# Loading r of the first three chunks on ACT's DMA queue in a recurrent attention and cosine MoE kernel

## The chip, the cores and the metric

The kernel runs on one core of one Trainium2 chip. The metric is the device time of one execution in microseconds. Engines are called PE (matmul), DVE (vector), ACT (activation), POOL (GpSimd) and SP (which only issues DMAs here). DMAs can be issued from the queues of SP, ACT and POOL.

## The reference

Two parts follow one another. The first is a linear recurrence over 768 time steps for 4 batches and 8 heads of width 48, with a decay w and a bonus u:

```python
for t in range(S):
    cur = einsum('bhd,bhe->bhde', u[None] * k[:, :, t], v[:, :, t])
    y[:, :, t] = einsum('bhd,bhde->bhe', r[:, :, t], state + cur)
    state = w[None, :, :, None] * state + einsum('bhd,bhe->bhde', k[:, :, t], v[:, :, t])
```

Its output, 3,072 tokens by 384, is the x of the second part, with weights of 384 x 2,048 and 2,048 x 384:

```python
h = x @ w_in
g = h * cos(h)
return g @ w_out
```

All data are float32, but the weights are drawn as float64 and converted in the kernel.

## The kernel before, in words

**The attention part.** The 768 steps of each batch are cut into chunks of 128; there are 24 chunks, numbered so that chunk i belongs to batch i mod 4. Function `chunk` writes down the operations of one chunk. It loads r, k and v with time on the partitions. POOL forms r*k (line 882), multiplies it by u (line 935), and multiplies k by its decay table (line 892). PE transposes k and r (line 851), DVE and ACT bring them back with decay (lines 910, 921 and 930), PE forms the 128 x 128 scores (line 976), ACT writes the diagonal that comes from u (line 960), DVE puts the scores under a mask (line 981), and PE forms the output with v and the carried state (lines 996 and 1007) and the new state (line 1022). ACT and DVE split the output into a high and a low part, `xh` and `xl` (lines 1222 and 1227). The first 12 chunks (`EARLY`) go this way. The later 12 are loaded and multiplied in another form (`late`), which the change does not touch.

**The buffers of the early chunks.** r has a ring of four buffers (`X_r`), k and v have six each (`R_k` with `X_k`, `R_v` with `X_v`), besides others that all chunks share.

**The MoE part.** Tokens go in eight blocks of three chunks. A step is one block and one of the 16 slices of 128 of the hidden width: nine matmuls for h (line 314), whole periods taken off on ACT and DVE (lines 326 and 329), the cosine with ACT's Sin function (line 332), the product with h (line 1330), a split into high and low (lines 1333 and 1336), and nine matmuls for the output (line 321). Each weight slice is loaded as raw 64-bit words (lines 550 and 571), put together from integers on ACT, DVE and POOL (lines 664 to 695), and split into high and low (lines 705 and 712); function `conv` writes this down. The first twelve chunks make up the first four blocks, and these are worked through four groups of slices.

**What sets the order.** Nothing is issued as it is written down. Every piece of work is given to a planner with `op(engine, due, cost, emit, after, bufs, ...)`. The planner plays the engines through in time with the costs written in the code: on each engine, of the pieces that could start first, it picks the one with the earliest due time. It makes seven passes (`PASSES`), in which due times are replaced by the latest time at which a piece may start, and keeps the pass that ends first by its own reckoning. The resulting order is then fixed on every engine's queue. Pieces that share a `line` are kept in the order in which they are written down, and `behind` keeps a piece behind another. A piece with a `dma` cost also waits for room on a modelled common transfer line. Where PE is to stand idle in the first part by this reckoning, warm-up matmuls are put in (line 1396). `CHUNK_SHIFT` and `TILE_SHIFT` are added to the due times of the 24 chunks and the 32 weight tiles; they were found by a search.

**The queues at the start.** All loads are on SP's queue. It issues w (line 447), then u (line 522), then the chunks' loads: r and k of an early chunk in two halves each (`load_p`, line 781), v in one (line 773). Loads of r, k and v are kept behind u (`behind=o_u`). ACT has nothing to do until it copies the decay table `dec_k` (line 513), except that it runs one Sin on a single element (line 281), which brings its function table in.

Of the kernel before, what the change touches and what calls it, by code (L numbers as in the profile page):

```python
# [14 lines left out]
AF = mybir.ActivationFunctionType  # L15
# [20 lines left out]
ON_DVE = (0, 0, 0)  # L36
RAW_K = 2
EARLY = 12

CHUNK_SHIFT = (  # L40
    -29.5, -37.6, -6.2, -7.2, 3.0, 2.3, 2.1, 0.6, 0.7, 1.4, 4.4, 4.6, -6.7, -104.0, -50.4, 0.8,
    -55.8, -62.5, -102.0, -6.5, -17.7, -92.4, 6.3, -24.8,
)
TILE_SHIFT = (
    -8.6, 5.5, -10.8, -48.0, -4.3, -6.4, -0.2, -16.4, 11.6, -5.1, 12.1, 2.5, 3.8, -0.3, 3.2, -0.8,
    14.0, 22.6, -2.8, 2.9, 12.9, -1.4, -0.8, 53.9, -8.3, 6.4, 1.2, 83.9, -13.0, -11.3, 2.5, 17.4,
)
PASSES = 7
DMA_AHEAD, DMA_FIRST, DMA_LAST, DMA_LAND = 3.0, 1.3, 0.6, 1.95
# [36 lines left out]
class Plan:  # L86
# [9 lines left out]
    def op(self, eng, due, cost, emit, after=(), bufs=(), lat=0.2, line=None, port=False, dma=0.0, behind=None):  # L96

        o = Op(eng, due, cost, lat, emit, after, bufs, self.lines.get(line) if line else behind, port, dma)
        if line:
            self.lines[line] = o  # L100
        self.ops.append(o)
        return o
# [137 lines left out]
def kernel(  # L240
# [11 lines left out]
    nc = tc.nc  # L252
# [25 lines left out]

    tiny = const.tile([1, 1], F32, name="tiny")
    nc.vector.memset(tiny, 0.0)  # L280
    nc.scalar.activation(tiny, tiny, AF.Sin)

    ident = const.tile([P, P], F32, name="ident")
    flag = const.tile([1, 1], I32, name="flag")
# [50 lines left out]
    with ExitStack() as actx:  # L335
# [63 lines left out]
        op = plan.op  # L399
        PE, DVE, ACT, POOL, SP, ACTQ = "PE", "DVE", "ACT", "POOL", "SP", "ACTQ"  # L400
# [33 lines left out]
        def wr():  # L434
# [15 lines left out]
            lat=2.6,  # L450
# [13 lines left out]
                )  # L464

        op(PE, -300, 2.4, start_banks, [o_dve], b_0)

        o_wT = op(PE, -95, 0.2, lambda: nc.tensor.transpose(b_w()[:, 0:NP], b_row()[0:NP, 0 : 2 * DP], ident[0:NP, 0:NP]), [o_w, o_wr, o_pool], [b_w, b_row], lat=0.3)

# [41 lines left out]
        def tab_copy():  # L511
# [6 lines left out]
        o_u = op(  # L518
            SP,
            -23.9,  # L520
            0.5,
            lambda: nc.sync.dma_start(u_b.rearrange("p h d -> p (h d)"), u.rearrange("h d -> (h d)").partition_broadcast(P)),
            lat=2.0,
            dma=0.6,
            behind=o_w,
        )
# [226 lines left out]
        def chunk(i, due, xbuf):  # L753
            b, c = i % B, i // B
            first = i < RAW_K
            bk = B_EARLY if i < EARLY else B_ATT

            def on(which):
                return (DVE, 0.47, nc.vector) if i < ON_DVE[which] else (POOL, 1.05, nc.gpsimd)
            mb, ab = Buf(R_f), Buf(R_a)  # L760
            if i < EARLY:
                rb, kb, vb = Buf(X_r), Buf(R_k + X_k), Buf(R_v + X_v)
            else:
                rb, kb, vb = Buf(R_f), Buf(R_k), Buf(R_v)
            trp = Buf(B_TR)
            R_Tc = R_T + X_T if i < EARLY else R_T
            kT, rT = Buf(R_Tc), Buf(R_Tc)
# [4 lines left out]
            def load(buf, src):  # L772
                return lambda: nc.sync.dma_start(
                    buf()[:, :, 0:D], src[b, :, c * C : (c + 1) * C, :].rearrange("h t d -> t h d")
                )


            def load_p(buf, src):
                def go():
                    for j in range(2):  # L780
                        nc.sync.dma_start(  # L781
                            buf()[:, j::2, 0:D],
                            src[b, j * NP : (j + 1) * NP, c * C : (c + 1) * C, :].rearrange("h t d -> t h d"),
                        )

                return go
# [10 lines left out]

            late = i >= EARLY
            if late:
                ks, rs = Buf(R_raw), Buf(R_raw)  # L800

            rbs = [rb]
# [31 lines left out]
            ahead = [last_A[0]] if late else []  # L834
            ln = "late" if late else None
            if late:
                l_ks = op(SP, due - 6.2, 1.9, load_s(ks, k), ahead, [ks], line=ln, dma=1.45)
                l_rs = op(SP, due - 6.1, 1.9, load_s(rs, r), ahead, [rs], line=ln, dma=1.45)
            l_k = op(SP, due - 5.2, 0.5 if late else 1.15, (load if late else load_p)(kb, k), ahead, [kb], line=ln, dma=1.25, behind=o_u)
            l_r = op(SP, due - 5.1, 0.5 if late else 1.15, load_r if late else load_p(rb, r), ahead, rbs, line=ln, dma=1.25, behind=o_u)  # L840
            l_v = op(SP, due - 5.0, 0.6, load(vb, v), ahead, [vb], line=ln, dma=1.25, behind=o_u)


# [52 lines left out]
            if not late:  # L896
# [7 lines left out]
                    lat=0.3,  # L904
# [341 lines left out]
        for i in range(NJ):  # L1246
            n = block_of[i]
            t = i - FIRST[n]
            if i < EARLY:
                due = -1.5 * (EARLY - i) - 1.0  # L1250
            else:
                lo, hi = first_h[n - 1], first_h[n] - 1
                if i >= XS:
                    lo = max(lo, last_h[block_of[i - XS]])
                due = lo + (hi - lo) * (t + 1) / BLOCKS[n]
            due = round(due, 2)
            due += CHUNK_SHIFT[i]
            x_ready.setdefault(n, []).extend(chunk(i, due, xb[i]))
            x_ready_of[i] = x_ready[n][-1]
# [4 lines left out]
        for i in range(2 * NF):  # L1264
            f, part = divmod(i, 2)
            g = max(x for x in group if x <= f)
            if g == 0:
                due = 2 * i - 3.0
            else:
# [3 lines left out]
                due = lo + (hi - lo) * (i - 2 * g + 1) / n_g  # L1273
            due = round(due, 2)
# [16 lines left out]
        for s, (n, f, f0, f1) in enumerate(steps):  # L1291
# [56 lines left out]
            for t in range(nt):  # L1348
# [8 lines left out]
                if f == f1 - 1:  # L1357
# [16 lines left out]
                    def st(ob=ob, dst=dst, f0=f0, last=last):  # L1374
# [14 lines left out]
                        dma=0.6 if f0 == 0 else 1.0,  # L1389
# [160 lines left out]
```

## Time and profile before

| | |
|---|---|
| times of three runs | 511.3, 509.42, 510.1 us |
| median | 510.1 us |
| time of the profiled execution | 510.29 us |
| its span, first to last instruction | 508.7 us |
| mean granted TensorE clock | 0.999 |
| PE busy | 497.1 us (98% of the span) |
| transfers of all queues | 61.82 MB |

The span is the time from the first instruction to the last, and the profiled execution's own time is a little longer. Busy shares are averages over the whole span. "L882" is line 882 of the kernel. A bracket behind an instruction tells how long its engine had stood idle and what ended that, and "SPq" and "ACTq" are the DMA issues on the queues of SP and ACT. [...]

### The profile page before, as it was taken

The page shows a single profiled execution, that of the slowest core. Times are in us where ns is not written, and L with a number is a line of the kernel's source. Part 1 is how long each engine was busy: PE and PEld are TensorE (multiplying, and loading weights), DVE is VectorE, ACT ScalarE, POOL GpSimd, SP SyncE. Part 2 cuts the span into 40 slices and gives each one's busy share as a digit, 9 for nine tenths or more (in the row PEclk, how much of TensorE's full clock was granted, in tenths as well). Part 3 has the DMA queues.
Part 4 walks back from the last instruction along what each step waited for, and adds up shares of the span by engine and source line. Part 5 has one row for each costly group of instructions (what it writes and reads, how often), then busy time and mean ns, then how long its engine had stood idle before and what let it go on. Part 6 is the DMA issues. An engine that isn't in the chain of part 4 may idle for free.

```text
span 508.7 us, 14928 instructions
## 1 busy us (share of the span) xinstructions
PE 497.1 (98%) x5872; PEld 474.7 (93%) x5872; DVE 396.0 (78%) x836; ACT 316.3 (62%) x805; POOL 176.3 (35%) x183
## 2 busy tenths in 40 slices
PE   8998999999999999999999999999999999999995
PEld 6876799999999999999999999999999999999994
DVE  6887888898998889798656678988888865566553
ACT  2886867767676676555755565655766655554443
POOL 6968312245434646364220144443224500000000
PEclk9999999999999999999999999999999999999999
DMA  9978525467946868672543938667765252010001
GB/s 139 158 144 175 136 84 179 165 129 141 178 129 130 181 134 182 123 150 71 111 77 95 156 97 212 151 154 190 189 155 130 75 173 64 0 48 3 0 1 52
DMA packets 116657, 61.82 MB, mean 122 GB/s; under 512 B 80097, under 2 KB 112482, under 8 KB 116578
## 3 DMA queue, kind: packets, MB, share of 16 engines
q1 hardware_dynamic: 110962, 53.11, 43.0%
q0 software_dynamic: 5184, 7.08, 10.1%
q8 instruction: 48, 0.79, 0.7%
q10 hardware_dynamic: 432, 0.59, 0.3%
q14 instruction: 31, 0.25, 0.2%
HBM read 48.96 MB, written 11.80 MB: 119 GB/s over the span
## 4 chain that ended last, share of the span: by engine, by line
PE 88%; SPq 4%; DMA 3%; POOL 3%; issue 1%; ACT 0%; DVE 0%; ACTq 0%; POOLq 0%
PE psum L321 40%; PE psum L314 39%; PE psum L1153 4%; SPq L781 2%; DMA early_r<-in_r_dram 2%; PE psum L1078 1%; PE psum L1094 1%; DMA early_k<-in_k_dram 1%; POOL f L935 1%; POOL f L882 1%; PE psum L1007 1%; DMA k<-in_k_dram 1%; SPq L550 1%; POOL k L892 1%; PE psum L996 1%
## 5 line engine op out<-in xcount | busy, mean ns | idle before, releaser
L321 PE MATMUL psum<-w_out_hi,gh 128*128 128x384 f32 x384 | 131.6, 343 | 0.0
L314 PE MATMUL psum<-xh,w_in_hi 128*128 128x384 f32 x384 | 129.9, 338 | 0.0
L321 PE MATMUL psum<-w_out_hi,gl 128*128 128x384 f32 x384 | 129.3, 337 | 0.0
L321 PE MATMUL psum<-w_out_lo,gh 128*128 128x384 f32 x384 | 129.3, 337 | 0.0
L314 PE MATMUL psum<-xh,w_in_lo 128*128 128x384 f32 x384 | 129.3, 337 | 0.0
L314 PE MATMUL psum<-xl,w_in_hi 128*128 128x384 f32 x384 | 129.0, 336 | 0.0
L1333 ACT CAST gh<-f 128x384 fp32r<-128x384 f32 (+1 forms) x132 | 66.0, 502 | 56.3 <-PE psum L321 33.8
L1336 DVE TENSOR_TENSOR gl<-f,gh 128x384 fp32r<-128x384 f32 (+1 forms) x132 | 83.2, 636 | 20.6 <-ACT gh L1333 20.0
L329 DVE SCALAR_TENSOR_TENSOR f<-psum,qi 128x384 f32<-128x384 f32 (+1 forms) x132 | 71.0, 540 | 34.7 <-ACT qi L326 34.2
L326 ACT ACTIVATE qi<-psum 128x384 int32<-128x384 f32 (+1 forms) x132 | 62.8, 478 | 49.5 <-PE psum L314 48.9
L332 ACT ACTIVATE f<-f 128x384 f32<-128x384 f32 (+1 forms) x132 | 67.5, 513 | 30.7 <-DVE f L329 29.5
L1330 DVE TENSOR_TENSOR f<-psum,f 128x384 f32<-128x384 f32 (+1 forms) x132 | 71.0, 540 | 17.0 <-ACT f L332 14.4
L321 PEld LDWEIGHTS psum<-w_out_hi,gh 128*128 128x128 f32 x384 | 72.0, 188 | 2.0 <-ACT f L1365 0.3
L314 PEld LDWEIGHTS psum<-xh,w_in_hi 128*128 128x128 f32 x384 | 72.1, 188 | 0.8 <-DVE f L329 0.2
L314 PEld LDWEIGHTS psum<-xl,w_in_hi 128*128 128x128 f32 x384 | 72.2, 188 | 0.0
L314 PEld LDWEIGHTS psum<-xh,w_in_lo 128*128 128x128 f32 x384 | 72.2, 188 | 0.0
L321 PEld LDWEIGHTS psum<-w_out_hi,gl 128*128 128x128 f32 x384 | 72.1, 188 | 0.0
L321 PEld LDWEIGHTS psum<-w_out_lo,gh 128*128 128x128 f32 x384 | 72.1, 188 | 0.0
L695 POOL TENSOR_TENSOR f<-f,raw 128x384 int32<-128x384 int32 x32 | 37.2, 1166 | 71.6 <-ACT f L332 19.4
L1380 POOL DMA_DIRECT2D out_dram<-f x36 | 33.6, 1071 | 55.0 <-ACT f L1365 47.4
L870 POOL TENSOR_TENSOR T<-T,decT_k 112x512 f32<-112x512 f32 x12 | 15.6, 1303 | 78.3 <-DVE T L865 70.1
L935 POOL TENSOR_TENSOR f<-f,u_b 128x384 f32<-128x384 f32 x24 | 26.9, 1122 | 0.2
(127 smaller groups left out, 627.8 us busy)
## 6 DMA issues: line engine op xcount, KB each, us to landing
raw<-in_moe_w_out_dram SPq DMA_DIRECT2D x32, 384.0 KB, 3.4
out_dram<-f POOLq DMA_DIRECT2D x36, 192.0 KB, 4.9
raw<-in_moe_w_in_dram SPq DMA_DIRECT2D x96, 64.0 KB, 2.3
raw<-in_moe_w_in_dram SPq DMA_DIRECT2D x16, 384.0 KB, 4.6
raw<-in_k_dram SPq DMA_DIRECT2D x47, 96.0 KB, 3.3
raw<-in_r_dram SPq DMA_DIRECT2D x47, 96.0 KB, 2.8
out_dram<-f SPq DMA_DIRECT2D x21, 192.0 KB, 2.2
v<-in_v_dram SPq DMA_DIRECT2D x18, 192.0 KB, 4.2
```

What stands on the lines that cost most here:

```text
L314: nc.tensor.matmul(ph, a, b_, start=(i == 0), stop=(i == len(mm) - 1))
L321: nc.tensor.matmul(acc, a[:, ts], b_, start=(first and i == 0), stop=(last and i == 2))
L326: nc.scalar.activation(qi, ph, AF.Copy, scale=INV_2PI, bias=0.25)
L329: nc.vector.scalar_tensor_tensor(q, ph, INV_2PI, qi, op0=ALU.mult, op1=ALU.subtract)
L332: nc.scalar.activation(q, q, AF.Sin, scale=TWO_PI, bias=0.5 * math.pi)
L695: lambda: nc.gpsimd.tensor_tensor(ai(), ai(), cn(), op=ALU.add),
L935: e1, due - 2.2, c1, lambda: n1.tensor_tensor(heads(mb), heads(mb), u_b, op=ALU.mult), [o_m, o_u], [mb], port=True
L1153: nc.tensor.matmul(xv()[rows, kk, tokens(n)] if same else apart(rows, kk), lhsT, rhs, start=quadrant not in opened, stop=True, skip_group_ ...
L1330: nc.vector.tensor_tensor(g()[:, cs], ph()[:, cs], q()[:, cs], op=ALU.mult)
L1333: nc.scalar.copy(gh()[:, cs], g()[:, cs])
L1336: nc.vector.tensor_tensor(gl()[:, cs], g()[:, cs], f32(gh())[:, cs], op=ALU.subtract)
L1380: nc.gpsimd.dma_start(dst, ob(), accum_op=ALU.add)
```

## The change

The loads of r for the first three chunks are issued from ACT's queue instead of SP's, in one line (chunk 0, 1, 2), with a due time ahead of everything else. The loads of k for these chunks stay on SP, with a due time 30 us earlier than before, and are no longer kept behind u. The Sin that brings ACT's function table in, which stood at the very start, becomes a piece for the planner that comes behind the r load of the second chunk. The shifts of chunks and tiles were searched anew.

```diff
+BOTH = 3

 CHUNK_SHIFT = (
-    -29.5, -37.6, -6.2, -7.2, 3.0, 2.3, 2.1, 0.6, 0.7, 1.4, 4.4, 4.6, -6.7, -104.0, -50.4, 0.8,
-    -55.8, -62.5, -102.0, -6.5, -17.7, -92.4, 6.3, -24.8,
+    -46.9, -67.3, -0.9, -1.6, 2.9, 1.8, 3.5, 4.5, 6.0, 7.9, 7.7, 9.6, -6.8, -110.2, -76.9, 1.4,
+    -86.2, -21.4, -56.0, -6.5, -17.8, -61.4, 22.7, -32.5,
 )
 TILE_SHIFT = (
-    -8.6, 5.5, -10.8, -48.0, -4.3, -6.4, -0.2, -16.4, 11.6, -5.1, 12.1, 2.5, 3.8, -0.3, 3.2, -0.8,
-    14.0, 22.6, -2.8, 2.9, 12.9, -1.4, -0.8, 53.9, -8.3, 6.4, 1.2, 83.9, -13.0, -11.3, 2.5, 17.4,
+    -2.0, 4.1, -3.5, -56.1, -11.7, -0.5, -11.9, -17.3, 0.8, -2.4, 8.8, 1.7, 4.5, 6.6, 1.3, -1.3,
+    13.1, 14.2, -7.2, 2.4, 12.2, -2.4, -8.6, 51.6, -5.7, 12.5, 4.4, 64.6, -13.1, -12.8, 12.2, 49.0,
 )
...
     nc.vector.memset(tiny, 0.0)
-    nc.scalar.activation(tiny, tiny, AF.Sin)
...
         op(PE, -300, 2.4, start_banks, [o_dve], b_0)
+        o_sin = op(ACT, -150, 1.5, lambda: nc.scalar.activation(tiny, tiny, AF.Sin))
...
-            def load_p(buf, src):
+            def load_p(buf, src, js=(0, 1), eng=nc.sync):
                 def go():
-                    for j in range(2):
-                        nc.sync.dma_start(
+                    for j in js:
+                        eng.dma_start(
                             buf()[:, j::2, 0:D],
                             src[b, j * NP : (j + 1) * NP, c * C : (c + 1) * C, :].rearrange("h t d -> t h d"),
                         )
...
-            l_k = op(SP, due - 5.2, 0.5 if late else 1.15, (load if late else load_p)(kb, k), ahead, [kb], line=ln, dma=1.25, behind=o_u)
-            l_r = op(SP, due - 5.1, 0.5 if late else 1.15, load_r if late else load_p(rb, r), ahead, rbs, line=ln, dma=1.25, behind=o_u)
+            if i < BOTH:
+                l_k = op(SP, due - 35.2, 1.1, load_p(kb, k), [], [kb], dma=1.2)
+                l_r = op(ACT, -300 + i, 1.1, load_p(rb, r, eng=nc.scalar), [], rbs, line="first", dma=0.1, lat=2.0)
+                if i == 1:
+                    o_sin.after.append(l_r)
+            else:
+                l_k = op(SP, due - 5.2, 0.5 if late else 1.15, (load if late else load_p)(kb, k), ahead, [kb], line=ln, dma=1.25, behind=o_u)
+                l_r = op(SP, due - 5.1, 0.5 if late else 1.15, load_r if late else load_p(rb, r), ahead, rbs, line=ln, dma=1.25, behind=o_u)
```

## The prediction

> **What bounds the kernel now.** I read the page's totals first, then the busy time by stretches, then the first 60 us engine by engine.
>
> ```profile
> span 508.7 us, 14928 instructions
> ## 1 busy us (share of the span) xinstructions
> PE 497.1 (98%) x5872; PEld 474.7 (93%) x5872; DVE 396.0 (78%) x836; ACT 316.3 (62%) x805; POOL 176.3 (35%) x183
> ```
>
> The profiled execution took 510.29 us, so 1.59 us lie outside its span. The median of the three runs shown is 510.1, so the sum below is made against 510.29 and stands 0.2 above the median. The 98% for PE is an average and counts warm-up matmuls as busy, so I cut the span where PE's idle gaps end, in the windows view (start:end, length, then each engine's busy us and count, granted clock, DMA share, GB/s):
>
> ```profile
> 0.00:5.80 5.80, 4.69 (x18) 2.42 (x19) 4.13 (x29) 1.49 (x2) 3.50 (x17) 1.00 0.57 109
> 5.80:33.90 28.10, 27.37 (x547) 22.45 (x547) 21.63 (x41) 19.39 (x58) 24.18 (x24) 1.00 1.05 149
> 33.90:59.24 25.34, 21.71 (x523) 17.39 (x519) 20.15 (x42) 20.02 (x59) 14.09 (x14) 1.00 0.82 168
> 59.24:502.60 443.36, 443.34 (x4792) 432.41 (x4792) 349.95 (x726) 274.93 (x687) 134.52 (x128) 1.00 0.50 117
> 502.60:508.70 6.10, 0.03 (x1) 0.00 (x0) 0.11 (x1) 0.48 (x1) 0.00 (x0) 0.89 0.31 107
> ```
>
> From 59.24 to 502.60 PE is busy 443.34 of 443.36 us at full clock. Nothing that moves loads or changes the order can win there, unless work is drawn into the first stage. The last 6.10 us are the final copies and stores, which the diff does not touch. So the change is worth what it does to the first 59.24 us, and a microsecond by which the full stretch starts earlier is a microsecond of the whole.
>
> In that stage PE is idle 59.24 - (4.69 + 27.37 + 21.71) = 5.47 us, and part of its busy time is filler:
>
> ```profile
> L1396 PE MATMUL psum<-warm 128*128 128x256 bf16 x101 | 14.8, 287 | 1.1 <-DVE f L437 1.1
> ```
>
> Warm-ups and idle together are some 20 us. That is what an ideal start could give at most, and it shows that PE does not set the pace. POOL does for a long stretch: three products per early chunk (r*k at L882, times u at L935, k times decay at L892).
>
> ```profile
> 7.22 1.01 POOL L882 TENSOR_TENSOR f<-early_r,k 128x384 f32<-128x384 f32 x1 [2.72 <-DMA k<-in_k_dram]
> 8.31 1.72 POOL L935 TENSOR_TENSOR f<-f,u_b 128x384 f32<-128x384 f32 x1
> 10.00 1.00 POOL L882 TENSOR_TENSOR f<-early_r,k 128x384 f32<-128x384 f32 x1
> 12.04 1.01 POOL L882 TENSOR_TENSOR f<-early_r,k 128x384 f32<-128x384 f32 x1 [1.03 <-DMA k<-in_k_dram]
> ```
>
> ```profile
> 12.04:33.90 21.86, 20.48 (x21) 1.00 0.92 145
> ```
>
> POOL waits 2.72 us for the first k and 1.03 for the third, and from 12.04 to 33.90 it is busy 20.48 of 21.86 us. In that stretch the chunks come out as fast as POOL multiplies. What makes its first and third product start earlier moves this whole stretch; two later waits I come to below.
>
> **The change part by part.** SP's queue now issues w, then u, then r and k in turn (start, length, count):
>
> ```profile
> 0.84 0.38 SPq L447 DMA_DIRECT2D f<-in_w_dram  x1
> 1.27 0.36 SPq L522 DMA_DIRECT2D u_b<-in_u_dram  x1
> 1.68 0.98 SPq L781 DMA_DIRECT2D early_r<-in_r_dram  x2
> 2.70 2.24 SPq L781 DMA_DIRECT2D k<-in_k_dram  x4
> 4.98 2.15 SPq L781 DMA_DIRECT2D early_r<-in_r_dram  x4
> 7.18 1.06 SPq L781 DMA_DIRECT2D k<-in_k_dram  x2
> 8.29 1.13 SPq L781 DMA_DIRECT2D early_r<-in_r_dram  x2
> ...
> 14.37 2.50 SPq L781 DMA_DIRECT2D early_r<-in_r_dram  x2
> ```
>
> A pair of issues costs 1.02 us of the queue (1.68 to 2.70). The change takes three such pairs off SP, 3.06 us, and lets the k of these chunks go ahead of u (their k is no longer tied behind u, and its due time is 30 us earlier).
>
> *What ACT pays.* It issues r of two chunks, loads its table, issues the third.
>
> ```profile
> 0.83 1.28 ACT L281 ACT_TABLE_LOAD   x1 [0.83 <-PEq L1535]
> 2.13 0.20 ACT L281 ACTIVATE tiny<-tiny 1x1 f32<-1x1 f32 x1
> 10.51 0.48 ACT L513 COPY dec_k<-psum 128x384 f32<-128x384 f32 x1 [8.18 <-PE psum L509]
> ```
>
> ```profile
> 502.14 0.76 ACTq L1376 DMA_DIRECT2D out_dram<-f  x1
> ```
>
> Six issues at SP's 0.51 are 3.06 us, with the table and the tiny Sin 1.5: ACT is free again at 0.83 + 4.6 = 5.4. At the one price of ACT's queue in this trace, 0.76 for a store, it is 0.83 + 4.56 + 1.5 = 6.9. Both lie inside the 8.18 us of idle time before 10.51, so the move costs nothing, and would still cost nothing if that copy came up by 3 us. The Sin that is moved has no reader before the cosines of the MoE.
>
> *When the first pair lands.* A load of half a chunk's r or k moves 96 KB, u's moves 192 (count, KB each, us to landing):
>
> ```profile
> early_r<-in_r_dram SPq DMA_DIRECT2D x24, 96.0 KB, 4.1
> ...
> u_b<-in_u_dram SPq DMA_DIRECT2D x1, 192.0 KB
> ```
>
> Before, 192 KB of u, 192 of r and 192 of k go out ahead of the first product. Now r leaves from ACT at 0.83 and the first k from SP at 1.27, its second half issued by 2.3 instead of 3.72. What the transfer engines did in those microseconds (window, clock, share, GB/s):
>
> ```profile
> 2.00:3.00 1.00, 1.00 0.32 97
> 3.00:4.00 1.00, 1.00 0.63 148
> 4.00:5.00 1.00, 1.00 1.21 241
> 5.00:6.00 1.00, 1.00 1.46 178
> ...
> 14.00:16.00 2.00, 1.00 1.46 167
> 16.00:18.00 2.00, 1.00 0.68 108
> ```
>
> Until 4 us they are half empty (share 0.32, 0.63 against 1.46 when full), so the first pair is held by its issue: at most 3.72 - 2.3 = 1.4 us to gain. By bytes, u's 192 KB (0.197 MB) less in front are 0.8 us at 241 GB/s or 1.2 us at 167. Against this, the loads of the second pair now enter the rings at the same time. For the third product, which waits until 12.04, the bytes through its k are 1,344 KB before and 1,152 KB after: 1.2 us at 167 GB/s, and the first issue is 0.44 earlier (0.83 against 1.27), 1.6 together.
>
> *What u pays.* Behind the k of three chunks its issue moves from 1.27 to 1.27 + 3.06 = 4.3, and with 1,152 KB ahead it lands near 10 to 11, where the first multiplication by u ran at 8.31. Behind that multiplication on POOL stand all later products. POOL then has two products done at about 10.8 instead of three at 12.04: of the 1.2 us up to one operation, 1.0, can be lost again. So the start is worth between 0.2 and 1.6 us; I take 1.2, the figure that the bytes give twice, because the trace shows POOL waiting for just these two k.
>
> [...]
>
> *The stall at 14.37.* The r pair there takes 2.50 us instead of 1.02: 1.5 us of waiting for an r buffer (there are four) behind POOL. The transfer rate falls from 167 to 108 GB/s, 2 us x 59/167 = 0.7 us of transfer lost. SP now comes to that point up to 3 us earlier and POOL frees the buffer earlier; loads that need no such buffer can be put in between. Between 0 and 0.7; I take 0.6, as 3 us in hand are more than the 1.5 of the stall.
>
> *The new shifts* change dues of all chunks and tiles, hence the order on every queue. In the full stretch nothing is to be had. In the first stage they can close or open waits, and the trace cannot show which; I take zero, and price both signs as rivals.
>
> The sum: 510.29 - 1.2 - 0.6 = **508.5 us**. With the ends above, 0.2 to 2.3 us, this case spans 508.0 to 510.1; the scatter of an unclaimed small wait either way makes it 507.3 to 510.3.
>
> **The rivals.** Their prices are two later waits of POOL and one block of SP:
>
> ```profile
> 24.02 1.01 POOL L882 TENSOR_TENSOR f<-early_r,early_k 128x384 f32<-128x384 f32 x1 [1.27 <-DMA early_r<-in_r_dram]
> ```
>
> ```profile
> 38.47 1.01 POOL L882 TENSOR_TENSOR f<-early_r,k 128x384 f32<-128x384 f32 x1 [4.61 <-DMA k<-in_k_dram]
> ```
>
> ```profile
> 28.31 3.16 SPq L550 DMA_DIRECT2D raw<-in_moe_w_in_dram  x6
> ```
>
> *The new order closes a later wait too.* The six weight loads at 28.31 hold SP 3.16 us just ahead of the chunk loads for which POOL waits 4.61 us. With 3 us in hand SP could pass them earlier. Against it: those chunk loads also wait for buffers that the chunks before free. With 1.27 of it, 508.5 - 1.3 = 507.2; with all 4.61, 503.9. I take 505.8, about the middle.
>
> *The new order puts weight loads or a blocked load ahead of chunk loads once more* (slower). Place: SP's queue, in order, with POOL behind it. Its price is a second wait like the one at 38.47: 508.5 + 4.61 = 513.1, or 514.9 if the start brings nothing. It decides the sign once the new wait exceeds the 1.8 us gained; to be seen as slower by over 0.5% it must exceed 1.6 + 2.5 = 4.1 us. For it: the order in before, from the same planner, left a wait of that size in this place. Against: SP has less to issue.
>
> *The transfers bind, not the issue:* the same bytes come at the same 167 GB/s, POOL waits elsewhere instead, and only the earlier first issue is left: 510.29 - 0.44 = 509.9, between 509.3 and 510.8. That the change does not do what it says, because r on ACT's ring and k on SP's slow one another until the first product is at 7.2 again, ends in the same place.
>
> **How the numbers follow.** Gain at the start alone 0.41; a later wait closed too 0.29; transfers bind 0.16; a new wait 0.14. A difference under 0.5%, 2.55 us, is about what a measurement of this kernel can't tell from no change; against the median that is 507.55 to 512.65. Faster takes in the second case nearly whole and a small end of the first, 0.27 + 0.06 = 0.33. Slower is the new wait, 0.14. The rest, 0.53, is no change to be told. The range leaves out the new wait (0.14) and the lowest end of the second case (about 0.05): from 504.6 to 511.6, where the upper end is the third case's 510.8 and 0.8 for the scatter of the runs.
>
> **What would show it.** Right: the first L882 starts near 6.0 and the third near 10.8; ACT's queue has six loads before 7 us and no wait for it behind them; the stretch in which PE never idles starts near 57.4 and is again about 443 us long. The u step is wrong if the first L935 starts before 9 us. The 14.37 step is wrong if SP still stands there over 1 us. The forecast is wrong if the full stretch begins after 59.2 although the first product is earlier, or if PE has gaps behind it, or if warm-ups and idle in the first stage are less by over 4 us, which only the new order could bring.

## The result, and the profile after

Before, the median is 511.0 us (9 runs, 509.4 to 513.4). After, it is 513.9 us (9 runs, 513.1 to 516.7). The ratio is 1.0075, with a 95% interval of 1.0053 to 1.0097: the changed kernel is slower, by some 3.8 us by the ratio (the medians lie 2.9 us apart), where 508.5 was forecast. The profiled execution took 515.4 us.

The page's totals of the kernel after:

```profile
span 513.6 us, 14925 instructions
PE 499.8 (97%) x5869; PEld 475.9 (93%) x5869; DVE 395.9 (77%) x836; ACT 315.9 (61%) x805; POOL 177.2 (35%) x183
```

The start did what it was meant to do, by half. POOL's and ACT's first work in the timeline after, with the issues on both queues (lines are 1 to 7 higher than before, so r*k is now L889, times u L942, k times decay L899):

```profile
0.83 4.11 ACTq L782 DMA_DIRECT2D early_r<-in_r_dram  x6
...
2.28 0.51 SPq L523 DMA_DIRECT2D u_b<-in_u_dram  x1
...
5.33 1.05 POOL L889 TENSOR_TENSOR f<-early_r,k 128x384 f32<-128x384 f32 x1 [0.81 <-DMA k<-in_k_dram]
...
6.27 0.20 ACT L467 ACTIVATE tiny<-tiny 1x1 f32<-1x1 f32 x1
...
7.64 2.02 POOL L942 TENSOR_TENSOR f<-f,u_b 128x384 f32<-128x384 f32 x1 [1.26 <-DMA u_b<-in_u_dram]
...
11.45 1.01 POOL L889 TENSOR_TENSOR f<-early_r,k 128x384 f32<-128x384 f32 x1 [0.49 <-DMA k<-in_k_dram]
...
12.77 0.48 ACT L514 COPY dec_k<-psum 128x384 f32<-128x384 f32 x1 [6.29 <-PE psum L510]
```

The first product starts at 5.33 instead of 7.22 and the third at 11.45 instead of 12.04. ACT is done with its loads and its table at 6.47 and idle for 6.29 us after that. Up to chunk 5 the lead even grows: its product starts at 22.10, where it was 24.02. Then POOL falls behind; the product of chunk 6 is 0.8 us later than before (timeline before):

```profile
26.92 1.02 POOL L882 TENSOR_TENSOR f<-early_r,k 128x384 f32<-128x384 f32 x1
```

Chunk 5's product and POOL's waits further on, in the timeline after:

```profile
22.10 1.01 POOL L889 TENSOR_TENSOR f<-early_r,early_k 128x384 f32<-128x384 f32 x1
...
27.74 1.01 POOL L889 TENSOR_TENSOR f<-early_r,k 128x384 f32<-128x384 f32 x1 [1.73 <-DMA k<-in_k_dram]
...
31.68 1.00 POOL L889 TENSOR_TENSOR f<-early_r,k 128x384 f32<-128x384 f32 x1 [2.93 <-DMA k<-in_k_dram]
...
46.40 1.01 POOL L889 TENSOR_TENSOR f<-early_r,early_k 128x384 f32<-128x384 f32 x1 [3.24 <-DMA early_r<-in_r_dram]
...
52.56 1.00 POOL L889 TENSOR_TENSOR f<-early_r,early_k 128x384 f32<-128x384 f32 x1 [2.12 <-DMA early_k<-in_k_dram]
```

These are the products of chunks 5, 6, 7, 10 and 11. In the kernel before the waits of this size were 1.27, 4.61 and 1.36 us, for chunks 5, 8 and 9. Chunk 11's wait passes on to PE, and there it costs more than its length (PE's timeline after, then two windows of PE: start:end, length, PE busy and count, granted clock, DMA share, GB/s; the share is the time of all packets over 16 engines, and it can be over 1: between 10 and 11 us of the kernel before it is 1.54):

```profile
54.89 0.44 PE L858 MATMUL psum<-ident,early_k 64*112 64x64 f32 x8 [1.90 <-POOL early_k L899]
...
59.39 0.45 PE L314 MATMUL psum<-xh,w_in_hi 128*128 128x384 f32 x1
```

```profile
51.80:55.21 3.41, 1.51 (x34) 1.00 0.91 231
55.21:58.62 3.41, 3.41 (x78) 0.50 0.48 128
```

Behind the 1.90 us of idle time the granted clock is 0.50 for 3.41 us: half of that, 1.70 us of PE's work, is lost. The first MoE step starts at 59.39, where it was at 42.05 before:

```profile
42.05 0.44 PE L314 MATMUL psum<-xh,w_in_hi 128*128 128x384 f32 x1
```

The windows by stage, after (start:end, length, then PE, PEld, DVE, ACT and POOL busy with counts, clock, DMA share, GB/s):

```profile
5.30:59.39 54.09, 50.02 (x1037) 39.41 (x1037) 40.15 (x76) 36.26 (x105) 38.87 (x38) 0.97 0.89 156
59.39:506.56 447.17, 447.05 (x4829) 435.57 (x4825) 351.98 (x733) 278.83 (x699) 134.84 (x128) 1.00 0.49 116
506.56:513.60 7.04, 0.00 (x0) 0.00 (x0) 0.07 (x1) 0.48 (x1) 0.00 (x0) 0.69 0.27 93
```

The full stretch begins at nearly the same time (59.39, before 59.24) but is 447.17 us long instead of 443.36, because 4,829 matmul records fall into it instead of 4,792 (8 of the 37 more are fillers, 1.0 us). PE has got less useful work done in the first 59 us. So the place to count is PE's time without useful work. In the first 100 us, filler matmuls, idle time, and what the clock loses (busy time times the missing share of the clock, by windows of 1 us) come to:

| kernel | filler | idle | clock | sum | PE's last matmul ends |
|---|---|---|---|---|---|
| before | 14.76 | 5.47 | 0 | 20.2 | 502.63 |
| after | 16.29 | 6.65 | 1.70 | 24.6 | 506.56 |

The sums differ by 4.4 us and PE's ends by 3.93. The rest of the 4.9 us between the spans is the tail of last stores, 7.04 us here and 6.07 before. The count is not complete, as a kernel further down (e11) shows: it leaves out what PE's useful matmuls themselves take longer in the records.

### The profile page after: what moved, and what is told of

The parts are those of the page before. It is cut to its first block, busy times and chain, and to the rows that moved or that the text cites. A ratio compares the mean times of both kernels' runs of the same rounds, so it can differ in the third digit from the quotient of the medians.

```text
span 513.6 us, 14925 instructions
## 1 busy us (share of the span) xinstructions
PE 499.8 (97%) x5869; PEld 475.9 (93%) x5869; DVE 395.9 (77%) x836; ACT 315.9 (61%) x805; POOL 177.2 (35%) x183
## 4 chain that ended last, share of the span: by engine, by line
PE 93%; DMA 1%; DVE 1%; ACT 1%; POOL 1%; issue 1%; DVEq 0%; POOLq 0%; ACTq 0%
PE psum L321 40%; PE psum L314 39%; PE psum L1160 4%; PE psum L1403 2%; PE psum L1014 2%; PE psum L1085 2%; PE psum L983 1%; PE psum L1101 1%; PE psum L858 1%; DMA k<-in_k_dram 1%; DMA early_k<-in_k_dram 1%; PE psum L1029 1%; PE psum L1003 1%; ACT T L967 0%; PE psum L458 0%
## 5 line engine op out<-in xcount | busy, mean ns | idle before, releaser
L1343 DVE TENSOR_TENSOR gl<-f,gh 128x384 fp32r<-128x384 f32 (+1 forms) x132 | 82.5, 633 | 20.6 <-ACT gh L1340 19.9
L1387 POOL DMA_DIRECT2D out_dram<-f x36 | 32.1, 1097 | 55.7 <-ACT f L1372 55.3
L942 POOL TENSOR_TENSOR f<-f,u_b 128x384 f32<-128x384 f32 x24 | 27.4, 1140 | 1.4 <-DMA u_b<-in_u_dram 1.3
```

What stands on the lines that cost most here:

```text
L942: e1, due - 2.2, c1, lambda: n1.tensor_tensor(heads(mb), heads(mb), u_b, op=ALU.mult), [o_m, o_u], [mb], port=True
L1343: nc.vector.tensor_tensor(gl()[:, cs], g()[:, cs], f32(gh())[:, cs], op=ALU.subtract)
L1387: nc.gpsimd.dma_start(dst, ob(), accum_op=ALU.add)
```

## The experiments

All ratios are to the kernel before on the same chip, with a 95% interval. Chunk and tile numbers count from 0.

**Is it the cold start of PE?** In the order after, PE's first transposes come earlier, so the planner leaves a longer gap behind them and fills it with 33 filler matmuls. They take 0.18 us each here (they start 0.21 us apart up to 10.8 us and 0.11 behind it), where a block of 19 took 0.12 us each in the kernel before, 2.24 us from 10.31 on (PE's timeline after):

```profile
6.34 5.96 PE L1403 MATMUL psum<-warm 128*128 128x256 bf16 x33
...
12.13 0.60 PE L510 MATMUL psum<-ident,decT_k 128*128 128x128 f32 x4
```

Before, the decay table was transposed at 9.87. Theory W takes these 2.3 us for the cause. e1_warm_ahead takes the delay out of the changed kernel, e2_before_delayed puts it into the kernel before:

```diff
 e1 (after)
+        early_n = dict(zip([o for o in order if o.eng == PE][2:4], (7, 19)))
+                    n = early_n.get(o, n)
 e2 (before)
+                    n += 19 * (o is o_tt)
```

> The changed kernel with its fillers on PE put elsewhere: 7 warm-up matmuls ahead of the first transposes (where it has none), and 19 instead of 33 ahead of the transposes of the decay table. Theory W (the block of 33 fillers, run at half speed for 5.96 us, holds PE's queue and makes the whole early chain some 2.3 us late): the first split of an output on ACT starts at 18.5 or earlier instead of 20.77, and the time falls by 2.3 to 4 us, to 510 to 511.6. Theory O (the new order puts weight loads ahead of chunk loads near 45 us, and that costs the time whatever the start does): the time stays within 0.8 us of 513.9. Theory Q (the two rings slow one another at the start): the same as O.

> The kernel before with 19 more fillers on PE ahead of the transposes of the decay table, some 2.25 us. Theory W: slower by 2.3 to 4 us, so 513.3 to 515. Theory O: POOL has the slack, the delay is absorbed, 511.0 to 511.8.

Measured: e1 513.69 us, 1.0078 (1.0062 to 1.0094); e2 510.45 us, 1.0011 (1.0002 to 1.002). W falls on both sides: without the delay nothing is won, and with it 0.1% is lost. In e1 the table was transposed 3.1 us earlier, at 8.99. POOL then waited as long for chunk 7's k as in the kernel after, and PE 3.85 us instead of 0.56 for chunk 6, whose k POOL multiplies behind that wait (timeline of e1):

```profile
8.99 0.60 PE L510 MATMUL psum<-ident,decT_k 128*128 128x128 f32 x4
...
32.06 0.99 POOL L889 TENSOR_TENSOR f<-early_r,k 128x384 f32<-128x384 f32 x1 [2.93 <-DMA k<-in_k_dram]
...
34.06 0.44 PE L858 MATMUL psum<-ident,k 64*112 64x64 f32 x8 [3.85 <-POOL k L899]
```

The k of chunk 7 came 0.4 us later than in the kernel after, although PE's chain of chunks had run 3 us ahead till then.

**Is it the queue or the order?** The change has two halves: r on ACT's queue, and new shifts, hence a new order. e3_shifts_only has the kernel before with the new shifts, and all loads on SP. e4_queue_only has the changed kernel with the old shifts. e5_before_order_r_on_act keeps the whole order of before, written out by the old plan, and only issues the three r loads from ACT:

```diff
 e5 (before)
-    nc.scalar.activation(tiny, tiny, AF.Sin)
+            l_r = op(SP, due - 5.1, 0.5 if late else 1.15, load_r if late else load_p(rb, r, nc.scalar if i < 3 else nc.sync), ahead, rbs, line=ln, dma=1.25, behind=o_u)
+                if o is o_dk:
+                    nc.scalar.activation(tiny, tiny, AF.Sin)
```

> The kernel before with the new shifts of chunks and tiles alone; all loads stay on SP and the Sin stays first. Theory O: slower by 2 to 4 us, 513 to 515, with a POOL wait of 2 us or more behind weight loads after 40 us. Theory W: 510.5 to 512, since the fillers at the start are those of before.

> The change without its new shifts: r of three chunks on ACT's queue, the Sin behind, the shifts of before. Theory W: the block of 33 fillers is there again, so at least 2.3 us slower than before, 513.3 or more. Theory O: no slower than before, 510 to 511.5. Theory Q: slower, with the third product on POOL no earlier than 12.0.

> The kernel before, planned and ordered as before, fillers as before; only r of the first three chunks is issued on ACT's queue instead of SP's, and the Sin stands ahead of ACT's first copy. Theory O (the whole loss is the new order of the queues, not the second ring): no slower than before, ratio 0.996 to 1.001. Theory Q (two rings slow one another): slower, ratio over 1.003.

Measured: e3 514.52 us, 1.0091 (1.0076 to 1.0107); e4 524.79 us, 1.0300 (1.0269 to 1.0332); e5 510.6 us, 1.0003 (0.9992 to 1.0014). Theory Q (the two queues cost) falls: with the order of before the queue alone costs nothing and brings nothing that the interval shows. O (the new order costs) holds for e3 and e5, as the new shifts alone cost as much as the whole change. For e4 O had 510 to 511.5 us and missed by far. Its start is as early as that of the kernel after (products at 5.59 and 11.37, where Q had the third at 12.0 or later), but every due time of the old search meets other neighbours in the changed list. So the two halves don't add up: the new shifts cost 0.9% on the old list, and the old shifts 3.0% on the new one. The cleanest comparison is the kernel after with e5, the same loads on the same queues in another order: 1.0075 and 1.0003. e5 also shows why the queue alone brings nothing (its timeline, then the waits of SP's queue up to 9.3 us: us in total, times, longest):

```profile
0.83 5.34 ACTq L780 DMA_DIRECT2D early_r<-in_r_dram  x6
...
1.68 5.70 SPq L780 DMA_DIRECT2D k<-in_k_dram  x6
...
7.76 1.00 POOL L881 TENSOR_TENSOR f<-early_r,k 128x384 f32<-128x384 f32 x1 [3.25 <-DMA k<-in_k_dram]
...
11.80 1.00 POOL L881 TENSOR_TENSOR f<-early_r,k 128x384 f32<-128x384 f32 x1 [0.27 <-DMA k<-in_k_dram]
```

```profile
SPq L780 <- DMA u_b<-in_u_dram: 1.3, 1, 1.3
SPq L780 <- DMA k<-in_k_dram: 1.1, 2, 0.9
SPq L780 <- DMA early_r<-in_r_dram: 1.0, 2, 0.8
```

Six k issues take SP 5.70 us here, where three pairs were 3.06, and the first product is 0.5 us later than before, the third 0.24 earlier. SP's queue stands 3.4 us in all until earlier loads have landed, and that is as much as the three pairs that were taken off it; the same view of the kernel before has no wait for a load. Nor do the transfers run faster: between 5 and 10 us they move 168 GB/s, and 167 in the kernel before. In the changed kernel such waits come to 3.2 us. That its first product starts at 5.33 all the same goes with the k of chunk 0 standing ahead of u, as in every kernel here that starts before 6 us; no run has this k ahead of u by itself.

In e3 the waits of POOL are smaller than before (1.29, 1.43 and 2.76 us), and it is slow all the same: PE has 16.82 us of fillers, 4.73 of idle time in the first 100 us, and among its waits is one of 1.61 us for `xh` from ACT at 56.15, after POOL's last long wait for a load. Another 1.92 us of PE's idle time come after 100 us, in the stretch where before there was next to none. So "POOL is late" is not the whole of it.

**Is it one place on SP?** In the order after, six issues of the second w_in tile stand ahead of chunk 11's k (SP's queue, after), as the slower rival of the prediction has it:

```profile
45.17 3.06 SPq L551 DMA_DIRECT2D raw<-in_moe_w_in_dram  x6
48.33 1.08 SPq L782 DMA_DIRECT2D early_k<-in_k_dram  x2
```

Also, six v loads stand ahead of chunk 6's k, where it was three. e6_tile_behind_k moves the tile's loads behind this k and a v, e7_v_behind_k the v loads of chunks 3 to 7 behind the k loads that they passed, e8_all_three both, with e1's fillers:

```diff
 e8 (after); e6 has the last pair alone, e7 the first five
+        sp = [o for o in order if o.eng == SP]
+        for o, to in [(14, 18), (15, 14), (17, 21), (20, 24), (23, 20), (32, 34)]:
+            order.remove(sp[o])
+            order.insert(order.index(sp[to]) + 1, sp[o])
```

> The changed kernel with one move on SP's queue: the six loads of the second w_in tile (issued at 45.17) go behind k of chunk 11 and v of chunk 9. Theory T (this tile ahead of k makes PE idle 1.9 us and then run at half clock for 3.4 us): that idle and the slow stretch vanish, and the time falls by 2.5 to 3.6 us, to 510.3 to 511.4. Theory V (the loss is made earlier, by v loads ahead of k): less than 1.2 us.

> The changed kernel with v of chunks 3 and 4 behind k of chunk 6, v of chunk 5 behind k of chunk 7, v of chunks 6 and 7 behind k of chunk 8. Theory V (v loads ahead of k starve POOL at 27.7 and 31.7): the two POOL waits of 1.73 and 2.93 us fall below 1 us each and the time falls by 1.5 to 4 us. Theory T: the two waits may go, but the time falls by less than 1 us, for the tile ahead of k of chunk 11 is still there.

> The changed kernel with the moves of both, the tile behind k and the v loads behind k, and with the fillers of 7 and 19 at the start. If the causes are the order of SP's queue and the block of fillers, and add up: 508.5 to 510.5, no slower than before. If something else in the new order binds (the first weight tile is converted later): 511.5 or more.

Measured: e6 515.58 us, 1.0100 (1.0068 to 1.0133); e7 515.72, 1.0110 (1.0084 to 1.0136); e8 515.51, 1.0086 (1.0067 to 1.0105). T and V both fall, and the moves don't add up either. In e7 chunk 6 has no such wait any more (its product is at 25.98), but POOL waits 3.68 us for chunk 7's k. In e6 the last r*k came 1.3 us earlier, but ACT, whose order is fixed, now stood at the tile's raw words, and PE behind it (timeline of e6):

```profile
53.11 0.55 ACT L665 ACTIVATE raw<-raw 128x384 int32<-128x384 uint32 x1 [3.75 <-DMA raw<-in_moe_w_in_dram]
...
55.80 0.68 PE L858 MATMUL psum<-ident,early_k 64*112 64x64 f32 x8 [2.49 <-issue]
```

The wait has gone to another engine and is no shorter there. None of the three kernels with moves on SP's queue is mended by them.

**Is it the clock, or an empty place in PE's queue?** e9_fill_gap puts 14 fillers into the 1.90 us gap, e10_warm_and_fill fills both gaps of e1, e12_first_h_ahead puts useful work there, the first MoE step:

```diff
 e9 (after)
+        hold = [o for o in order if o.eng == PE and o is order[246]]
+                    n += 14 if o in hold else 0
 e10 (e1)
+        hold = {order[147]: 28, order[246]: 16}
+                    n += hold.get(o, 0)
 e12 (after)
+        for o, to in [(order[224], order[241]), (order[252], order[243]), (order[260], order[252])]:
+            order.remove(o)
+            order.insert(order.index(to) + 1, o)
```

> The changed kernel with 14 more filler matmuls ahead of the transposes of chunk 11, where PE was idle for 1.90 us at 52.98 to 54.89 and the granted clock then fell to 0.50 for most of 55 to 59 us. The fillers need nothing that is late, so they take only idle time. Theory C (the idle time makes the clock fall, and the 1.7 us of PE time so lost are part of the loss): the clock stays at 1.00 from 55 to 59, PE's last matmul ends near 504.9 instead of 506.56, the median is 512.2, ratio to the kernel before 1.004 (1.002 to 1.006). Rival D (the clock falls for another reason than this gap, as what runs beside it): the clock falls again between 55 and 59 and the ratio stays 1.0075. Rival E (PE at full clock then waits for its operands, as POOL is late anyway): clock 1.00, PE's idle time after 55 us grows by the 1.7, ratio 1.0075.

> The changed kernel with its start warmed earlier as in e1_warm_ahead (7 fillers ahead of the first transposes, 19 instead of 33 ahead of the decay table's), and fillers in the two idle times of PE that this left: 28 ahead of the transposes of chunk 6 (3.85 us idle, clock 0.50 to 0.78 behind it) and 16 ahead of those of chunk 11 (2.20 us). Theory C: no clock drop, so 1.7 us of e1_warm_ahead come back and nothing more: PE ends near 504.1, median 512.0, ratio 1.004. The rest of the loss stays, as POOL's waits for r and k are not touched. Rival D or E: 513.7, ratio 1.0078. If the waits followed from the cold start too, all would be gone: 1.000.

> The changed kernel with three moves in its order: PE's first MoE step (nine matmuls, 3 us) stands ahead of chunk 11's transposes instead of behind that chunk's outputs; for that, DVE writes the low part of the first w_in tile ahead of the masks and the state of chunk 10 and 11, and ACT casts the first tile's high part ahead of the second tile's raw, for whose load it waited 1.08 us. Theory P (PE's fixed order is the cause: it stands at chunk 11's transposes, idle, and the clock falls, while useful work could run): the nine matmuls start between 53 and 54.5 instead of 59.39 and fill the idle time of 1.90 us; no clock drop (1.7 us); chunk 11 comes about 1 us later; PE ends near 503 to 504, median 510.0 to 511.5, ratio 0.999 to 1.002. Rival V (as with the fillers, PE waits for the next late thing instead): PE's idle time moves behind the step, ratio 1.005 to 1.0075.

Measured: e9 514.84 us, 1.0064 (1.0041 to 1.0087); e10 514.58, 1.0078 (1.0049 to 1.0106); e12 514.56, 1.0086 (1.0071 to 1.0102). In e12 the step writes the PSUM bank in which scores of a late chunk still wait for their mask, so that those scores are replaced by the step's sums; the instructions are the same. The clock in e9 (windows of PE):

```profile
55.00:56.00 1.00, 0.00 (x0) 1.00 1.00 313
56.00:57.00 1.00, 0.99 (x47) 1.00 1.19 293
57.00:58.00 1.00, 1.00 (x54) 1.00 1.06 323
```

It stays at 1.00, and PE waits all the same: k and r of chunks 10 and 11 came 1.3 us later in this execution than in that of the kernel after, with the same loads in the same order. For chunk 10, 0.65 us of this is a later issue on SP (43.11, in the kernel after 42.46) (timeline of e9):

```profile
47.72 1.01 POOL L889 TENSOR_TENSOR f<-early_r,early_k 128x384 f32<-128x384 f32 x1 [4.14 <-DMA early_r<-in_r_dram]
...
56.01 0.44 PE L858 MATMUL psum<-ident,early_k 64*112 64x64 f32 x8 [1.06 <-POOL early_k L899]
```

In e12 the step filled the gap as planned, from 53.46 on, but in its profiled execution the clock fell to 0.50 after 34 us instead, behind another wait of PE for POOL, which stood at chunk 7's k. Theory C's ratio of 1.004 for e10 lies outside the interval, for e9 just outside. So with the gaps filled the clock did not fall (1.00 in the first 100 us of e9 and of e10), as C has it and D has not, but its loss comes and goes with the waits; a fixed 1.7 us of the difference it is not. The mean clock over all runs says the same: in e3 and e9 its median is 0.997, next to 0.998 and 0.997 in the kernel before beside them, and they are slower by 0.9 and 0.6%. P falls as well.

**Is it what the planner was told?** In the changed list the r loads on ACT's queue are charged 0.1 on the planner's transfer line, where the same load on SP is charged 1.25. e11_charged_searched charges them in full and has the shifts searched anew; e13_charged_warm takes fillers out of its start:

```diff
 e11 (after; with new CHUNK_SHIFT and TILE_SHIFT)
-                l_k = op(SP, due - 35.2, 1.1, load_p(kb, k), [], [kb], dma=1.2)
-                l_r = op(ACT, -300 + i, 1.1, load_p(rb, r, eng=nc.scalar), [], rbs, line="first", dma=0.1, lat=2.0)
+                l_k = op(SP, due - 35.2, 1.1, load_p(kb, k), [], [kb], dma=1.25)
+                l_r = op(ACT, -300 + i, 1.1, load_p(rb, r, eng=nc.scalar), [], rbs, line="first", dma=1.25, lat=2.0)
 e13 (e11)
+        early_n = dict(zip([o for o in order if o.eng == PE][2:4], (7, 16)))
+                    n = early_n.get(o, n)
```

> The changed kernel, but in the planner's list the r loads of the first three chunks, which leave from ACT's queue, are charged on the transfer line at 1.25 each, as their k is, instead of 0.1 (k 1.25 instead of 1.2), and the due shifts are searched anew with that. In the order that comes out, the last k stands ahead of the second w_in tile on SP, k6 to k8 stand ahead of the v loads that passed them, and 27 fillers instead of 33 stand ahead of the decay table's transposes. Theory U (the loss comes from an order made for loads that land sooner than the chip delivers them, because transfers from ACT's queue were taken as free): POOL's idle time between its third product and its last falls from 10.89 us to that of the kernel before, 7.5, or less; its last product ends by 53.5 instead of 56.1; no clock drop; with the early start kept the median is between 509.5 and 511.5, ratio 0.998 to 1.002. Rival A (the transfers set the last product whatever the order; the early start only makes POOL wait longer later): POOL's idle time stays near 10.9, its last product near 56, ratio 1.0075. Rival B (other due shifts of the same kind, other places of the waits): the wait moves to ACT or PE as in the hand moves before, ratio 1.005 to 1.012.

> The kernel with the r loads charged and the shifts searched anew (e11_charged_searched), with 7 fillers instead of 4 ahead of the first transposes and 16 instead of 27 ahead of the decay table's, so that the table is transposed at about 9.9 instead of 11.48 us. Theory L (behind 27 us the loads set the pace, and a start of PE that is 1.5 us earlier only waits longer for them): ratio to the kernel before as in e11_charged_searched, 1.000 (0.998 to 1.002). Rival S (the cold fillers were the last thing that kept the early start from counting): PE ends 1.0 to 1.5 us earlier than in e11_charged_searched, ratio 0.997 to 0.998.

Measured: e11 510.98 us, 1.0005 (0.998 to 1.003), the loss is gone; e13 510.53, 1.0015 (0.9998 to 1.0031), no more than that, so L holds and S falls. The expectation of e11 misread its list in one point: the second w_in tile still stands ahead of the last k there. And U's time came true without U's steps (POOL and PE of e11):

```profile
30.60 1.00 POOL L889 TENSOR_TENSOR f<-early_r,k 128x384 f32<-128x384 f32 x1 [2.24 <-DMA early_r<-in_r_dram]
...
44.68 1.02 POOL L889 TENSOR_TENSOR f<-early_r,early_k 128x384 f32<-128x384 f32 x1 [4.13 <-DVE early_T L988]
...
53.20 1.01 POOL L889 TENSOR_TENSOR f<-early_r,early_k 128x384 f32<-128x384 f32 x1 [1.69 <-DMA early_r<-in_r_dram]
```

```profile
53.00:60.00 7.00, 7.00 (x175) 1.00 0.67 172
```

Chunk 6's and chunk 7's long waits for k are gone, but POOL waits as long in other places and its last product is as late (it starts at 55.26, in the kernel after at 54.80). The difference is on PE, which is busy throughout where it stood idle in the kernel after: 15.25 us of fillers, 3.29 of idle time, no clock loss, 18.5 together. Here the count of PE's lost time shows its limit. The sum is 1.7 us less than in the kernel before, yet PE's last matmul ends at 503.26, 0.6 us later: the useful matmuls themselves take 2.3 us longer in the records, spread over many lines. Why, no run shows.

**Was it the charge, or the search?** e11 differs from the kernel after in both. So two orders were searched as long without the charge, and a second one with it (only the shifts differ, so there is no diff to show):

> The changed kernel with other due shifts alone: searched anew as long as for e11_charged_searched, but with the r loads on ACT's queue taken as nearly free as in the changed kernel (0.1). The planner reckons its order to end at 497.6 us, where it reckons 499.2 for the changed kernel, 498.6 for the kernel before and 497.9 for e11_charged_searched (numbers of the planner, not of the chip). Theory U (the uncharged loads make every such order late): ratio 1.005 to 1.010, k6 and k7 waited for by POOL over 1.5 us each as in the changed kernel. Rival R (the changed kernel's shifts are only a poor order, already by the planner's own reckoning; any order that it reckons 1.5 us shorter gives the loss back, charged or not): ratio 0.996 to 1.002.

> A second order of the same kind as e14_searched_uncharged_1, from another start of the random search; the planner reckons 497.8 us. Theory U: 1.005 to 1.010. Rival R: 0.996 to 1.002. If the two differ by more than 0.5% from one another, what an order gives on the chip is spread wider than either theory says.

> A second order with the r loads charged at 1.25, from another start of the search; the planner reckons 498.1 us, 0.2 more than for e11_charged_searched. Theory U: as there, 0.998 to 1.003. Rival R: the same, 0.998 to 1.003. If it is above 1.005, the charge was not what helped in e11_charged_searched.

All orders together, by the end that the planner reckons for each (its own number, from the costs in the code, no measurement) and by what the chip made of it. The medians come from several chips; the ratios are each to the kernel before on the same chip:

| kernel | r loads charged | planner's end | median, us | ratio |
|---|---|---|---|---|
| e14 | no | 497.6 | 512.62 | 1.0061 (1.0033 to 1.0089) |
| e15 | no | 497.8 | 517.74 | 1.0137 (1.0112 to 1.0161) |
| e11 | yes | 497.9 | 510.98 | 1.0005 (0.998 to 1.003) |
| e16 | yes | 498.1 | 517.17 | 1.0131 (1.0098 to 1.0163) |
| before | all on SP | 498.6 | 511.0 | 1 |
| after | no | 499.2 | 513.9 | 1.0075 (1.0053 to 1.0097) |
| e3 | all on SP | 499.5 | 514.52 | 1.0091 (1.0076 to 1.0107) |
| e4 | no | 507.0 | 524.79 | 1.0300 (1.0269 to 1.0332) |

Both U and R fall. With the charge one order is at 1.0005 and the other at 1.0131; without it 1.0061 and 1.0137. Four orders that the planner puts within 0.5 us of one another lie some 6.7 us apart on the chip, by their ratios. Only a difference of 8 us in its reckoning (e4) shows. The planner itself put the kernel after 0.6 us behind the kernel before, which needs no chip to be seen. In e15 and e16 some of the loss is outside the first stage, where the forecast saw nothing to be lost (windows of PE and a wait of e15; then windows of e16):

```profile
140.00:160.00 20.00, 19.31 (x110) 1.00 0.76 166
160.00:180.00 20.00, 17.91 (x151) 0.91 0.46 101
```

```profile
162.09 0.44 PE L321 MATMUL psum<-w_out_hi,gl 128*128 128x384 f32 x1 [2.78 <-DVE gl L1343]
```

```profile
56.00:64.00 8.00, 7.60 (x61) 0.57 0.55 125
200.00:220.00 20.00, 18.87 (x108) 1.00 0.73 148
```

In e15 PE waits 2.78 us for `gl` in the middle of the full stretch and the clock falls again behind it (0.91 in the mean of 160 to 180 us).

## Why the prediction was wrong

**What bounds the kernel: right, but not the yardstick.** The full stretch is PE's, and a matmul not done before it is done in it. The prediction measured the change by the start of this stretch and took its length as fixed. The start moved by only 0.15 us; the loss is in the length, 3.8 us more, for work that the first stage left over (1.0 us of it are fillers). The sign that the prediction named for its own failure came, a full stretch that begins after 59.2 although the first product is earlier.

**ACT pays nothing: right.** All six loads went ahead of the table, not four of them. Loads and table end at 6.47 us, inside the 5.4 to 6.9 that were worked out, though 1.1 us of it is a wait of the sixth load (issued at 4.57), which the working did not have.

**The start, 1.2 us: right in direction, half in size.** The third product is 0.6 us earlier (11.45, forecast 10.8). Of the two reasons given, the issue was none. The prediction held the first pair back "by its issue" and took 3.06 us off SP; in e5 the second half of the first k is issued at 2.15 instead of 3.25, and the first product starts at 7.76 instead of 7.22, and the time taken off SP comes back as waits for loads to land. The order of k and u is the reason that is left. u itself was read wrongly: it was issued third, at 2.28, and not behind the k of three chunks at 4.3, so the first multiplication by it started at 7.64 and not after 9.

**The stall at 14.37, 0.6 us: right in part.** The r pair of chunk 4 takes 1.05 us, from 13.64 on, and between 14 and 18 us the transfers run at 180 and 129 GB/s instead of 167 and 108. But the k pair behind it takes 1.4 us more than the 1.02 of a pair that waits for nothing (SP's queue after). The view of SP's waits puts 0.3 us at most of that to another engine, so what holds it is not settled:

```profile
15.40 2.46 SPq L782 DMA_DIRECT2D early_k<-in_k_dram  x2
```

**The new shifts, taken as zero: the step that failed.** On the old list they cost 0.91% by themselves (e3), about 4.6 us, and the changed kernel differs from e5, whose r is on ACT's queue too, by 0.7%, some 3.7 us. Either is more than all terms of the sum. The prediction reasoned that the trace can't show what a new order does, and then took the middle and gave the side of a new wait a chance of 0.14. That was too small: of the seven other planned orders run here none is shown to be faster, one is as fast, and six are slower by 0.6% to 3%. This suggests that the order before was not a draw like any other; what its search went by is not on record. Against such an order an early start of 0.6 us weighs little.

**The slower rival: right in sign and size (513.1, measured 513.9), wrong in its mechanism.** Six weight loads do stand ahead of a chunk load and POOL waits 2.12 us behind them, less than the 4.1 that it was to exceed. Moving them (e6) gives nothing back. As far as the runs show, the loss lies in several small waits that hand over to one another; no run takes them out one by one.

**Transfers that bind: true of the queue alone.** That rival has the same bytes come at the same 167 GB/s when ACT issues a part of them. e5 agrees (1.0003, and 168 against 167 GB/s): the transfers were not delivered sooner because two engines issued them. Nor was issuing time saved on SP's queue, because of the waits in e5 (six k issues in 5.70 us, where three pairs were 3.06).

**What stays open.** Why the chip takes 12.4 us more than the planner reckons in one order (before, 511.0 against 498.6) and 19.9 in another (e15) is not settled. It isn't the cold start, the queue, one load on SP, the clock's drop or the charge of the r loads, each by itself. That POOL gets the same load 1.3 us later in another execution with the same order of loads (46.40 and 47.72 above) makes it likely that short slack in the order counts, but this was only argued.

## What to carry to other kernels

A change that has the order of a tuned kernel searched anew is two changes, and they are to be costed and tested apart: here r on the second queue, with the old order, was worth nothing measurable, and the new order cost 0.7 to 0.9%. Where a planner's reckoning and the chip differ by more than the orders do from each other, the best order by the plan is little better than a random draw, so several have to be timed on the chip before the edit is judged. Before a load is moved to another queue to save issuing time, look whether the queue is held by its issues or by loads that have not landed. And when one wait is taken out of an order that is fixed on every engine, look first for the next engine that stands at it.

## What the runs showed of the hardware

**The granted clock fell behind some idle times of PE and not behind others.** In the kernel after it was 0.50 for 3.41 us (55.21 to 58.62), which lost 1.70 us; in e1, e7 and e13 the loss was 1.70 again, and in e16 3.35, as it was down there for some 6.8 us. The length of one gap does not decide it in these runs. The clock fell after gaps of 1.11 (e13), 1.32 (e12), 1.90 (after), 2.14 (e7) and 3.85 us (e1), and did not fall after 1.61 (e3), 1.70 (e14), 1.76 (e9) and 2.20 (e1). What else decides it, no run here shows.

**A second queue puts no more loads on the way in this program.** In the records of the loads on SP's and ACT's queues (before and after) each names one of eight semaphores in turn, and an issue that takes one up again waits until the load that had it before has landed. So at most eight of these loads are under way, whichever queue issues them. In the kernel before this costs nothing at the start: an issue of half a chunk takes 0.51 us, eight take some 4.1, and a load lands 3.8 us after its issue (the k issued at 4.43 at 8.27, and the issue that needs it to have landed comes at 8.87). One queue keeps eight loads under way by itself. In the kernel after two queues issue, and SP's issues at 5.19 and 7.52 come 0.02 us behind the landing of k (5.17) and of u (7.50). The issues themselves are not slower there: those two take 0.37 us each.
